# First norm's modulation columns by TensorE alone from a 128-row layout of w_mod; x tiles by two queues in turn; V begins with four row tiles

## The chip, the cores and the metric

The kernel runs on one core of a Trainium2 chip. The metric is device time in microseconds of one execution. Before the change it is 1380.65 us, the median of 3 runs (1380.23 to 1380.73). All instructions of an engine run in the order in which they are written; engines wait for each other through semaphores, and DMA transfers are issued from the queues of SyncE (SP) and ScalarE (ACT).

## The reference, cut to what matters

The input x has 2048 rows of 448. The condition c has 448 elements. With D = 448:

```
mod = (silu(c) @ w_mod).reshape(1, 6, 1, D)      # w_mod: 448 x 2688
sa, ca, ga, sb, cb, gb = mod[:, 0..5]
h = layernorm(x) * (1 + ca) + sa
q, k, v = heads of h @ wqkv                       # wqkv: 448 x 1344, 16 heads of 28
x = x + ga * (softmax(q k^T * 28**-0.5) v) @ wo
h = layernorm(x) * (1 + cb) + sb
x = x + gb * mlp(h)                               # gMLP with a spatial product
```

The change is about the first norm: its two modulation vectors sa and ca, the row tiles of x that it needs first, and the product h @ wqkv for v that follows.

## The kernel before, in words

The schedule is written out by hand: every engine executes in the order of the source. The kernel has a short beginning (norm, transposes, V, Q and K for the four groups of 512 rows), a long attention stage, an output projection, and a gMLP stage.

What happens in the first group (rows 0 to 511, four row tiles of 128):

- **Loads.** SP issues `cc_t` (c as 112 x 4, L266), then `load_x(0)` (L239; row tiles 0 and 1 go by ACT's queue, 2 and 3 together by SP), then `load_mod(0)` (L234): four tiles `wm` of 112 x 2 x 448, k = 0 to 3, each with the columns of sa and ca for 112 of the 448 rows of w_mod. Then come the four row blocks of the V part of wqkv (L250; the last block has 64 rows and is loaded twice, into both halves, by `load_z`, L145 and L146), and the next four row tiles of x.
- **Filling.** `pe_fill(n, with_)` (L288) puts n products of 128x128 that nobody reads on TensorE. Each float32 product is two LDWEIGHTS and two MATMULs in the trace, so `pe_fill(20, ones)` shows as 40 instructions. The float32r products of V show as one.
- **Norm.** VectorE takes the statistics of each row tile (L337, L338), GpSimd the reciprocal roots (L165, L166), VectorE normalizes (L348), ACT copies the last 64 columns a second time (L356). TensorE transposes (`tp_first`, L429): 8 transposes for two row tiles, 16 in all, into four banks `tp`, one for each 128 columns of h (the fourth holds the last 64 columns twice).
- **Modulation columns.** `cols["ca"]` and `cols["sa"]` hold 1+ca and sa as columns of 128 partitions. The sums over rows of w_mod are formed by ACT (k = 0, L438), VectorE (k = 1, 2, L299; the last step k = 3 in pieces, `mod_last`, L465) and then summed over the 112 partitions by TensorE with products of one moving column (`mod_dot`, L478). VectorE moves each column to SBUF (`mod_cols`, L485 and L487).
- **h and V.** For each column block c, `h_hi` (ACT, L499) writes the rounded h from `tp`, `h_full` (VectorE, L494) the full one, `h_lo` (L142) the remainder. `wv_hi` and `wv_lo` split the weight in the same way. V is the sum over 11 steps (`STEPS`), a step being one pair of an h part and a weight part; `v_step(j, kts)` (L535) does step j for the row tiles kts. Before, the first three steps run for row tiles 0 to 2 between the products for the columns c = 1 and c = 3, then for row tile 3, and then the rest for all four.
- **After V** come the products of Q and K (`qk_unit`, L381), which need the split weights of the parts "a" and "b". The tiles of part "a" reuse the buffers of `wm`, those of part "b" the buffers of the V weights, and so their loads wait until these have been read.

The same `load_mod`, `mod_acc`, `mod_split` and `mod_sum` serve the other four modulation vectors later (pairs 1 and 2).

Of the kernel before, what the change touches and what calls it, by code (L numbers as in the profile page):

```python
# [8 lines left out]
F32 = mybir.dt.float32  # L9
# [80 lines left out]
def tile_adaln_mha_gmlp(ctx, tc, x, wqkv, wo, w_in, w_spT, b_sp, w_out, cT, w_mod, out):  # L90
# [19 lines left out]
    dve.memset(ones, 1.0)  # L110
    mhalf = const.tile([128, 4], F32, name="mhalf")
    dve.memset(mhalf, -0.5)
    silu = const.tile([112, 4], F32, name="silu")
    cols = {}
    for nm in ("sa", "ca", "sb", "cb"):
        cols[nm] = const.tile([128, 4], F32, name=f"col_{nm}")
# [27 lines left out]
    def load_z(eng, dst, src):  # L144
        eng.dma_start(dst[0:64], src)  # L145
        eng.dma_start(dst[64:128], src)  # L146
# [68 lines left out]
    e2 = late_e.enter_context(tc.tile_pool(name="e2", bufs=1, side="right"))  # L215

    wv = e2.tile([128, 8, D], F32R, name="wv")
    ones_r = e2.tile([112, 128], F32R, name="ones_r")
    dve.memset(ones_r.bitcast(F32), 1.0)
    wms, xts, raws = {}, {}, {}  # L220

# [3 lines left out]
    def bank(name):  # L225
        k = mode[0](name) if mode[0] else banks[0]
        banks.remove(k)
        banks.append(k)
        return ring.tile([128, 512], F32, name=name, tag=f"b{k}")

    def load_mod(pair, eng):
        for k in range(4):
            wms[pair, k] = e1.tile([112, 2, D], F32, name="wm", tag=("wm", "wm", "raw")[pair], bufs=4)
            eng.dma_start(wms[pair, k], w_mod[:, pair, k])  # L234

    def load_x(g, eng):
        xg = e1.tile([128, 4, D], F32, name="xg")
        for t0, t1 in ((0, 1), (1, 2), (2, 4)) if g == 0 else ((0, 4),):
            (act if t1 - t0 == 1 else eng).dma_start(xg[:, t0:t1, :], x[g, :, t0:t1])  # L239
        for t in range(4):  # L240
            xts[4 * g + t] = xg[:, t, :]

# [3 lines left out]
    def load_w(kind, i, eng):  # L246
        c0, n, tag = PARTS[kind]
        raw = e1.tile([128, 2 * D], F32, name="raw", tag=tag, bufs=4)[:, :n]
        if i < 3:
            eng.dma_start(raw, wqkv[i * 128 : (i + 1) * 128, c0 : c0 + n])  # L250
        else:
            load_z(eng, raw, wqkv[384:448, c0 : c0 + n])
        raws[kind, i] = raw

    def qk_part(kind, i, eng):
# [6 lines left out]
        else:  # L262
            sub(eng, wqk[0:64, 7, cs], raw[0:64], wqk[0:64, 6, cs])

    cc_t = e1.tile([112, 4], F32, name="cc_t", bufs=1)
    sp.dma_start(cc_t, cT)  # L266
    load_x(0, sp)
    load_mod(0, sp)
# [5 lines left out]
    pool.memset(V[:, :, :, DH:32], 1.0)  # L274


    ec = e1.tile([112, 4], F32, name="ec", bufs=1)
    act.activation(ec, cc_t, AF.Exp, scale=-1.0)
    dve.tensor_scalar(out=ec, in0=ec, scalar1=1.0, scalar2=None, op0=ALU.add)
    dve.reciprocal(ec, ec)  # L280
    dve.tensor_tensor(out=silu, in0=cc_t, in1=ec, op=ALU.mult)

    pcs = {c: bank("pc") for c in (0, 2)}
    wu = bank("wu")

    def pe_fill(n, with_):
        for _ in range(n):
            pe.matmul(wu[:, 0:128], with_[:, 0:128], ones, start=True, stop=True)  # L288
# [2 lines left out]

    def mod_acc(pair, k):
        if k == 0:
            accs[pair] = e2.tile([112, 2, D], F32, name="acc")
        wm, acc = wms.pop((pair, k)), accs[pair]
        if k == 0:
            dve.tensor_scalar(out=acc, in0=wm, scalar1=silu[:, 0:1], scalar2=None, op0=ALU.mult)
        else:
            dve.scalar_tensor_tensor(out=acc, in0=wm, scalar=silu[:, k : k + 1], in1=acc, op0=ALU.mult, op1=ALU.add)  # L299

    def mod_split(pair, eng, pool_l, tag_l, bufs_l):

        acc = accs.pop(pair)
        accs[pair] = []
        for part in range(2):
            h = stage.tile([128, 512], F32R, name="acc_h", tag="qf")[0:112, :D]
            l = pool_l.tile([112, D], F32R, name="acc_l", tag=tag_l, bufs=bufs_l)
            act.activation(h, acc[:, part, :], AF.Copy)
            sub(eng, l, acc[:, part, :], h)
            accs[pair].append((h, l))  # L310
# [33 lines left out]
    def ln_norm(g, ts):  # L344
        mv, rs = mv1[g]
        for t in ts:
            xn = e1.tile([128, 512], F32, name="xn", bufs=4)
            dve.tensor_scalar(  # L348
                out=xn[:, :D],
                in0=xts.pop(4 * g + t),  # L350
                scalar1=mv[:, t, 0:1],
                scalar2=rs[:, t : t + 1],
                op0=ALU.subtract,
                op1=ALU.mult,
            )
            act.activation(xn[:, D:], xn[:, 384:D], AF.Copy)  # L356
            xn1.setdefault(g, []).append(xn)
# [56 lines left out]
    def wv_lo(i, eng):  # L414
        raw = raws.pop(("v", i))
        if i < 3:
            sub(eng, wv[:, 3 + i, :], raw, wv[:, i, :])
        else:
            sub(eng, wv[0:64, 7, :], raw[0:64], wv[0:64, 6, :])
# [7 lines left out]
    def tp_first(t):  # L427
        for c in range(4):
            pe.transpose(tps[c][:, t * 128 : (t + 1) * 128], xn1[0][t][:, c * 128 : (c + 1) * 128], ident)  # L429

    x3 = xts[3]
    pe_fill(20, ones)
    ln_stat(0, (0, 1))
    ln_rs(0, 0, 2)
    ln_stat(0, (2, 3))
    ln_rs(0, 2, 4)
    accs[0] = e2.tile([112, 2, D], F32, name="acc")
    act.activation(accs[0], wms.pop((0, 0)), AF.Copy, scale=silu[:, 0:1])  # L438
    ln_norm(0, (0, 1))
    mod_acc(0, 1)  # L440
    tp_first(0)
    tp_first(1)
    ln_norm(0, (2, 3))
    mod_acc(0, 2)
    pe_fill(5, x3)
    tp_first(2)
    tp_first(3)
    pe_fill(2, x3)

    acc0 = [stage.tile([128, 512], F32, name="acc0", tag="qh")[0:112] for _ in range(2)]  # L450
    wm3 = wms.pop((0, 3))

    def mod_last(c):
        for part in (1, 0):
            if c < 3:
                o = acc0[part][:, c * 128 : (c + 1) * 128]
                a, w = (v[:, part, c * 128 : (c + 1) * 128] for v in (accs[0], wm3))
            else:  # L460
                o = acc0[part][:, 384:512].rearrange("p (r n) -> p r n", n=64)
                a, w = (
                    v[:, part, 384:D].rearrange("p (r n) -> p r n", r=1).broadcast_to([112, 2, 64]) for v in (accs[0], wm3)
                )
            dve.scalar_tensor_tensor(out=o, in0=w, scalar=silu[:, 3:4], in1=a, op0=ALU.mult, op1=ALU.add)  # L465

    def mod_dot(c, which):
        if c == 1:
            pcs[c] = ps_o.tile([128, 512], F32, name="pc", tag="o")
        if c == 3:  # L470
            pcs[c] = pcs[1][:, 2:4]
        for i, part in enumerate((1, 0)):
            cs = slice(c * 128, (c + 1) * 128)
            if which == "C":
                o, lhs, rhs = 2 + i, wm3[:, part, cs], silu[:, 3:4]
            else:
                o, lhs, rhs = i, (accs[0][:, part] if which == "A" else acc0[part])[:, cs], ones[:112, 0:1]
            pe.matmul(pcs[c][:, o : o + 1], lhs, rhs, start=True, stop=True)  # L478

    def mod_cols(c):  # L480
        for i, (nm, plus1) in enumerate((("ca", 1.0), ("sa", 0.0))):
            o = cols[nm][:, c : c + 1]
            if c == 0:
                a, b = pcs[c][:, i : i + 1], pcs[c][:, 2 + i : 3 + i]
                dve.tensor_scalar(out=o, in0=a, scalar1=b, scalar2=plus1, op0=ALU.add, op1=ALU.add)  # L485
            else:
                dve.tensor_scalar(out=o, in0=pcs[c][:, i : i + 1], scalar1=plus1, scalar2=None, op0=ALU.add)  # L487

    def h_full(c):
        if c < 2:  # L490
            fs[c] = e1.tile([128, 512], F32, name="hfull")
        else:
            fs[c] = stage.tile([128, 512], F32, name="hfull", tag="qf")
        dve.tensor_scalar(  # L494
            out=fs[c], in0=tps[c], scalar1=cols["ca"][:, c : c + 1], scalar2=cols["sa"][:, c : c + 1], op0=ALU.mult, op1=ALU.add
        )

    def h_hi(c):
        act.activation(  # L499
# [10 lines left out]
        load_w("a", i, sp)  # L510
    wv_hi(0)
    wv_hi(2)
    mod_dot(0, "C")
    mod_dot(0, "A")
    mod_last(2)
    pe_fill(2, x3)
    mod_dot(2, "all")
    pe_fill(4, x3)
    mod_cols(0)
    h_hi(0)  # L520
    mod_cols(2)
    h_hi(2)
    mod_last(1)
    mod_last(3)
    wv_hi(1)
    wv_lo(0, dve)


    order = [STEPS[j] for j in (0, 1, 6, 2, 3, 4, 7, 5, 8, 9, 10)]
    pvs = [(kt, bank("pv") if kt < 3 else None) for kt in range(4)]  # L530

    def v_step(j, kts):
        a, b = order[j]
# [2 lines left out]
                pvs[kt][1][:, :D], hT[0][:, a, kt * 128 : (kt + 1) * 128], wv[:, b, :], start=j == 0, stop=j == NST - 1  # L536
            )

    v_step(0, (0, 1, 2))
    mod_dot(1, "all")  # L540
    mod_cols(1)
    h_hi(1)
    wv_hi(3)
    v_step(1, (0, 1, 2))
    mod_dot(3, "all")
    wv_lo(2, dve)
    h_full(0)
    mod_cols(3)
    h_hi(3)
    v_step(2, (0, 1, 2))  # L550
    pvs[3] = (3, ps_o.tile([128, 512], F32, name="pv", tag="o"))
    for j in range(3):
        v_step(j, (3,))
    h_lo(0, pool)
    h_full(2)
    h_full(1)
    wv_lo(1, dve)
    h_lo(2, dve)
    h_lo(1, dve)
    h_full(3)  # L560
    h_lo(3, dve)
    wv_lo(3, dve)
    load_x(2, sp)
    for i in (0, 2, 1, 3):
        load_w("b", i, sp)
    for j in range(3, NST):
        v_step(j, range(4))

    def qk_hi(i):
# [1042 lines left out]
```

## Time and profile before

| what | value |
|---|---|
| median of 3 runs | 1380.65 us |
| profiled execution: its own time | 1381.31 us |
| profiled execution: span of its instructions | 1379.5 us |
| TensorE busy (MATMUL) | 1373.1 us, 100% of the span |
| VectorE, ScalarE, GpSimd busy | 1072.2, 785.0, 357.8 us |
| granted TensorE clock | 1.0 |

The span is the time from the first to the last instruction of the profiled execution; 1.8 us of its own time lie around it. In the rows below PE is TensorE's MATMULs, PEld its LDWEIGHTS, DVE VectorE, ACT ScalarE, POOL GpSimd, SPq and ACTq the queues that issue DMAs. A row of the timeline has the start (us from the span's start), the length of a merged piece, engine, line, operation, output and inputs, and the number of instructions in it.

### The profile page before, as it was taken

To read this page: it belongs to the slowest core of one execution; us is meant where nothing else is said; L and a number is where in the kernel's file an instruction comes from. 1 tells how busy PE (TensorE), PEld (TensorE's weight loads), DVE (VectorE), ACT (ScalarE), POOL (GpSimd) and SP (SyncE) were. 2 spreads that over 40 slices of the span, in tenths; PEclk is the share of its full clock that TensorE was granted. 3 is DMA by queue.
4 is the path that set the end of the run, shared out by engine and by line. 5 is a ranking of instruction groups with operands and counts; after the bars stand their busy time and mean duration, and the time that the engine had idled before them with its cause. 6 is when DMAs were issued, how large, how long until landed. Compare 5 with 4: busy or idle time off the path is not lost.

```text
span 1379.5 us, 20122 instructions
## 1 busy us (share of the span) xinstructions
PE 1373.1 (100%) x7120; PEld 978.1 (71%) x7120; DVE 1072.2 (78%) x1727; ACT 785.0 (57%) x1451; POOL 357.8 (26%) x359
## 2 busy tenths in 40 slices
PE   9999999999999999999999999999999999999998
PEld 8888655555555555555555555888898888888898
DVE  7798888888888888888888880672268798889682
ACT  4724677777777777777777779364234654444221
POOL 2234324243325544633442302200042000000000
PEclk9999999999999999999999999999999999999999
DMA  8565633454244544542343321533202433335842
GB/s 253 167 157 191 201 91 111 109 157 136 89 117 122 161 121 129 156 134 90 109 122 80 108 58 49 174 141 127 85 0 76 130 100 114 116 92 179 269 160 80
DMA packets 93041, 174.56 MB, mean 127 GB/s; under 512 B 17032, under 2 KB 32010, under 8 KB 90394
## 3 DMA queue, kind: packets, MB, share of 16 engines
q1 hardware_dynamic: 90222, 168.97, 41.1%
q10 hardware_dynamic: 2718, 4.30, 0.9%
q8 instruction: 56, 0.92, 0.3%
q14 instruction: 45, 0.37, 0.1%
HBM read 111.61 MB, written 56.82 MB: 122 GB/s over the span
## 4 chain that ended last, share of the span: by engine, by line
PE 99%; DMA 0%; DVE 0%; ACT 0%; ACTq 0%; issue 0%
PE st_ps L724 19%; PE acc L1405 19%; PE o_ps L739 17%; PE mt L692 17%; PE z_ps L1297 5%; PE pq L381 5%; PE z_ps L1129 5%; PE wo_ps L995 3%; PE pv L363 2%; PE y_ps L1485 2%; PE y_ps L1484 2%; PE y_ps L1483 2%; PE tp L175 1%; PE pv L535 1%; DMA xg<-in_x_dram 0%; PE mtp L713 0%
## 5 line engine op out<-in xcount | busy, mean ns | idle before, releaser
L697 DVE TENSOR_REDUCE pm<-mt 128x1 f32<-128x512 f32 x1024 | 631.2, 682 | 86.0 <-PE mt L692 86.0
L728 ACT ACTIVATE P<-st_ps 128x512 f32<-128x512 f32 x1024 | 514.6, 631 | 202.0 <-PE st_ps L724 201.9
L724 PE MATMUL st_ps<-qst,kst 128*128 128x512 f32 x1024 | 404.5, 406 | 0.0
L692 PE MATMUL mt<-kst,qst 128*128 128x512 f32 x1024 | 402.5, 393 | 0.0
L724 PEld LDWEIGHTS st_ps<-qst,kst 128*128 128x128 f32 x1024 | 191.2, 187 | 141.3 <-issue 93.1
L739 PE MATMUL o_ps<-P,V 128*32 128x512 f32 x2048 | 247.1, 598 | 0.0
L1405 PE MATMUL acc<-wsp_h,heapA 128*128 128x512 f32 x752 | 231.5, 389 | 0.0
L692 PEld LDWEIGHTS mt<-kst,qst 128*128 128x128 f32 x1024 | 192.4, 188 | 31.6
L846 POOL TENSOR_TENSOR ws_raw<-ws_raw 128x512 f32<-128x512 f32 x124 | 159.2, 1287 | 190.8 <-DMA ws_scr<-ws_raw 129.2
L1405 PEld LDWEIGHTS acc<-wsp_h,heapA 128*128 128x128 f32 x752 | 141.2, 188 | 29.2
L1405 PE MATMUL acc<-wsp_l,heapA 128*128 128x512 f32 x376 | 146.3, 389 | 0.0
L739 PEld LDWEIGHTS o_ps<-P,V 128*32 128x32 f32 x2048 | 54.7, 109 | 123.0 <-issue 114.7
L1185 ACT ACTIVATE wsp_h<-raw_sp 128x512 fp32r<-128x512 f32 x104 | 65.6, 632 | 125.1 <-PE acc L1405 113.6
L142 DVE TENSOR_TENSOR wsp_l<-raw_sp,wsp_h 128x512 fp32r<-128x512 f32 x104 | 70.4, 686 | 16.6 <-ACT wsp_h L1185 16.4
L1405 PEld LDWEIGHTS acc<-wsp_l,heapA 128*128 128x128 f32 x376 | 70.6, 188 | 14.7
L381 PE MATMUL pq<-heapD,heapD 128*128 128x512 f32 x196 | 61.8, 390 | 0.0
L1301 DVE BATCH_NORM_STATS2 stz<-z 128x6 f32<-128x448 f32 x32 | 19.9, 626 | 44.6 <-ACT z L1300 44.5
L142 DVE TENSOR_TENSOR heapA<-z,heapA 128x1536 fp32r<-128x1536 f32 (+2 forms) x25 | 39.9, 1605 | 6.6 <-ACT heapA L1220 6.5
L1300 ACT ACTIVATE z<-z_ps 128x448 f32<-128x448 f32 x32 | 17.4, 543 | 47.4 <-PE z_ps L1297 47.4
L381 PEld LDWEIGHTS pq<-heapD,heapD 128*128 128x128 f32 x196 | 36.7, 188 | 7.5
L768 POOL TENSOR_TENSOR osb<-osb,rb 128x512 f32<-128x512 f32 x15 | 19.3, 1290 | 87.0 <-DMA rb<-r_scr 77.8
L1484 PE MATMUL y_ps<-wouts,uT 128*128 128x448 f32 x112 | 40.9, 365 | 0.0
(220 smaller groups left out, 1438.7 us busy)
## 6 DMA issues: line engine op xcount, KB each, us to landing
ws_scr<-ws_raw SPq DMA_DIRECT2D x92, 256.0 KB
raw_sp<-ws_scr SPq DMA_DIRECT2D x92, 256.0 KB
ws_raw<-in_w_spT_dram SPq DMA_DIRECT2D x72, 256.0 KB
kst<-qk_scr SPq DMA_DIRECT2D x45, 224.0 KB
qst<-qk_scr SPq DMA_DIRECT2D x45, 224.0 KB
qk_scr<-qh SPq DMA_DIRECT2D x28, 256.0 KB
qk_scr<-ql SPq DMA_DIRECT2D x28, 256.0 KB
z_scr<-z1t SPq DMA_DIRECT2D x28, 256.0 KB
```

The lines of the kernel that those rows point to most:

```text
L142: eng.tensor_tensor(out=dst, in0=a, in1=hi.bitcast(F32), op=ALU.subtract)
L381: pe.matmul(pq, wqk[:, b, m * 128 : (m + 1) * 128], hT[g][:, a, :], start=j == 0, stop=j == NST - 1)
L692: pe.matmul(mt, qst[h % 3][:, t * 128 : (t + 1) * 128], kst[h % 3][:, kb * 512 : (kb + 1) * 512], start=True, stop=True)
L697: dve.tensor_reduce(out=pms[h][:, t, kb : kb + 1], in_=mt, axis=AX.X, op=ALU.max)
L724: pe.matmul(st, kst[h % 3][:, kt * 128 : (kt + 1) * 128], qst[h % 3][:, qb * 512 : (qb + 1) * 512], start=True, stop=True)
L728: act.activation(p, st, AF.Exp, scale=SCALE)
L739: pe.matmul(otile[h][32 * qb : 32 * qb + 32, :], V[:, kt, h, :], ptiles.pop((u, qb)), start=kt == 0, stop=kt == NT - 1)
L846: pool.tensor_tensor(out=ws_tile(op[0]), in0=ws_tile(op[2]), in1=ws_tile(op[4]), op=ALU.add if op[3] == "+" else ALU.subtract)
L1129: pe.matmul(ps_t, w1[:, b, f * 128 : (f + 1) * 128], h2T[g][:, a, :], start=j == 0, stop=j == NST - 1)
L1297: pe.matmul(ps_t[:, :D], h2T[g][:, a, tt * 128 : (tt + 1) * 128], w2[:, b, hf * D : (hf + 1) * D], start=j == 0, stop=j == NST - 1)
L1405: pe.matmul(a[j], z[:, c], w, start=start and k == 0, stop=st == 3 and k == 2, skip_group_check=not new or j == 3)
L1484: pe.matmul(y[:, :D], uT[k][:, 7 + f, ts], wouts[0][:, f, :], start=False, stop=False)
```

## The change

- The host lays w_mod out in 128 rows: three tiles (k = 0, 1, 2) of 128 x 2 x 448, and a fourth with 448 columns in which the last 64 rows of w_mod stand for sa in partitions 0 to 63 and for ca in partitions 64 to 127. c is laid out as 128 x 4 to match, with its last 64 elements in both halves, and `silu` is 128 x 5: columns 3 and 4 hold the last 64 elements in the one and the other half, with zeros elsewhere. wqkv gets its last 64 rows twice on the host, so that its last block is one load of 128 rows.
- The columns sa and ca come from TensorE alone. `mod_dot(k)` multiplies the 128-column blocks of `wm` with the k-th column of `silu` and adds up over k in one bank `pc0`. The fourth block has 64 columns and is multiplied twice, into partitions 0 to 63 and 64 to 127. That makes 10 products for each of k = 0, 1, 2 and 5 for k = 3 (with two moving columns there). VectorE then moves all four columns of ca, and all four of sa, in one instruction each. `mod_last` and `mod_cols` are gone.
- The four row tiles of x are four loads: 0 and 2 by ACT's queue, 1 and 3 by SP's.
- The order on TensorE is: 26 fill products (20 before), `mod_dot(0)`, `mod_dot(1)`, the transposes of row tiles 0 and 1, `mod_dot(2)`, the transposes of 2 and 3, `mod_dot(3)`, 5 fill products, and then all 11 steps of V, each for four row tiles. `h_full` for c = 1 and 3 moves from VectorE to ACT. Steps 2 and 6 of V change places.
- For the later pairs `mod_acc` takes the last k in two halves.

```diff
-    silu = const.tile([112, 4], F32, name="silu")
+    silu = const.tile([128, 5], F32, name="silu")
+    pool.memset(silu, 0.0)
...
     def load_mod(pair, eng):
         for k in range(4):
-            wms[pair, k] = e1.tile([112, 2, D], F32, name="wm", tag=("wm", "wm", "raw")[pair], bufs=4)
-            eng.dma_start(wms[pair, k], w_mod[:, pair, k])
+            n = 2 if k < 3 else 1
+            wms[pair, k] = e1.tile([128, 2, D], F32, name="wm", tag=("wm", "wm", "raw")[pair], bufs=4)[:, :n]
+            eng.dma_start(wms[pair, k], w_mod[:, pair, 2 * k : 2 * k + n])
...
-        for t0, t1 in ((0, 1), (1, 2), (2, 4)) if g == 0 else ((0, 4),):
-            (act if t1 - t0 == 1 else eng).dma_start(xg[:, t0:t1, :], x[g, :, t0:t1])
+        for t0, t1 in ((0, 1), (1, 2), (2, 3), (3, 4)) if g == 0 else ((0, 4),):
+            (act if g == 0 and t0 % 2 == 0 else eng).dma_start(xg[:, t0:t1, :], x[g, :, t0:t1])
...
-        if i < 3:
-            eng.dma_start(raw, wqkv[i * 128 : (i + 1) * 128, c0 : c0 + n])
-        else:
-            load_z(eng, raw, wqkv[384:448, c0 : c0 + n])
+        eng.dma_start(raw, wqkv[i * 128 : (i + 1) * 128, c0 : c0 + n])
...
-    dve.tensor_tensor(out=silu, in0=cc_t, in1=ec, op=ALU.mult)
-    pcs = {c: bank("pc") for c in (0, 2)}
+    for r0, r1, a, o in ((0, 128, 0, 3), (0, 64, 3, 1), (64, 128, 3, 1)):
+        b = a + r0 // 64
+        dve.tensor_tensor(out=silu[r0:r1, b : b + o], in0=cc_t[r0:r1, a : a + o], in1=ec[r0:r1, a : a + o], op=ALU.mult)
...
+    pc0 = ps_o.tile([128, 512], F32, name="pc", tag="o")
+
+    def mod_dot(k):
+        wm = wms.pop((0, k))
+        for c in range(4):
+            for part in range(2 if k < 3 else 1):
+                w = wm[:, part, c * 128 : min(D, (c + 1) * 128)]
+                v = silu[:, k : k + 1] if k < 3 else silu[:, 3:5]
+                for r in (slice(0, 128),) if c < 3 else (slice(0, 64), slice(64, 128)):
+                    o = pc0[r, 2 * c + part : 2 * c + part + 1] if k < 3 else pc0[r, 2 * c : 2 * c + 2]
+                    pe.matmul(o, w, v, start=k + c + part == 0, stop=k == 3, skip_group_check=True)
+
-    pe_fill(20, ones)
+    pe_fill(26, ones)
     ln_stat(0, (0, 1))
     ln_rs(0, 0, 2)
     ln_stat(0, (2, 3))
     ln_rs(0, 2, 4)
-    accs[0] = e2.tile([112, 2, D], F32, name="acc")
-    act.activation(accs[0], wms.pop((0, 0)), AF.Copy, scale=silu[:, 0:1])
+    mod_dot(0)
+    mod_dot(1)
     ln_norm(0, (0, 1))
-    mod_acc(0, 1)
     tp_first(0)
     tp_first(1)
+    mod_dot(2)
     ln_norm(0, (2, 3))
-    mod_acc(0, 2)
-    pe_fill(5, x3)
     tp_first(2)
     tp_first(3)
-    pe_fill(2, x3)
+    mod_dot(3)
+    pe_fill(5, ones)
...
     wv_hi(0)
     wv_hi(2)
-    mod_dot(0, "C")
-    mod_dot(0, "A")
-    mod_last(2)
-    pe_fill(2, x3)
-    mod_dot(2, "all")
-    pe_fill(4, x3)
-    mod_cols(0)
+    wv_lo(0, dve)
+    for nm, part, plus1 in (("ca", 1, 1.0), ("sa", 0, 0.0)):
+        dve.tensor_scalar(out=cols[nm], in0=pc0[:, part:8:2], scalar1=plus1, scalar2=None, op0=ALU.add)
     h_hi(0)
-    mod_cols(2)
+    h_full(0)
     h_hi(2)
-    mod_last(1)
-    mod_last(3)
+    h_lo(0, pool)
+    wv_lo(2, dve)
     wv_hi(1)
-    wv_lo(0, dve)
-    order = [STEPS[j] for j in (0, 1, 6, 2, 3, 4, 7, 5, 8, 9, 10)]
-    pvs = [(kt, bank("pv") if kt < 3 else None) for kt in range(4)]
+    h_hi(1)
+    h_full(2)
+    wv_hi(3)
+    h_hi(3)
+    wv_lo(1, dve)
+    h_full(1, act)
+    h_lo(2, dve)
+    h_full(3, act)
+    h_lo(1, dve)
+    h_lo(3, dve)
+    wv_lo(3, dve)
+    order = [STEPS[j] for j in (0, 1, 2, 6, 3, 4, 7, 5, 8, 9, 10)]
+    pvs = [(kt, bank("pv") if kt < 3 else ps_o.tile([128, 512], F32, name="pv", tag="o")) for kt in range(4)]
...
     load_x(2, sp)
     for i in (0, 2, 1, 3):
         load_w("b", i, sp)
-    for j in range(3, NST):
+    for j in range(NST):
         v_step(j, range(4))
```

More of the change, by code (lines that the diff above doesn't have):

```diff
@@ L217, in tile_adaln_mha_gmlp @@
     wv = e2.tile([128, 8, D], F32R, name="wv")
-    ones_r = e2.tile([112, 128], F32R, name="ones_r")
+    ones_r = e2.tile([128, 128], F32R, name="ones_r")
     dve.memset(ones_r.bitcast(F32), 1.0)
@@ L263, in qk_lo @@
             sub(eng, wqk[0:64, 7, cs], raw[0:64], wqk[0:64, 6, cs])
-    cc_t = e1.tile([112, 4], F32, name="cc_t", bufs=1)
+    cc_t = e1.tile([128, 4], F32, name="cc_t", bufs=1)
     sp.dma_start(cc_t, cT)
@@ L274, in tile_adaln_mha_gmlp @@
     pool.memset(V[:, :, :, DH:32], 1.0)
-    ec = e1.tile([112, 4], F32, name="ec", bufs=1)
+    ec = e1.tile([128, 4], F32, name="ec", bufs=1)
     act.activation(ec, cc_t, AF.Exp, scale=-1.0)
@@ L293, in mod_acc @@
         if k == 0:
-            accs[pair] = e2.tile([112, 2, D], F32, name="acc")
+            accs[pair] = e2.tile([128, 2, D], F32, name="acc")
         wm, acc = wms.pop((pair, k)), accs[pair]
@@ L297, in mod_acc @@
             dve.tensor_scalar(out=acc, in0=wm, scalar1=silu[:, 0:1], scalar2=None, op0=ALU.mult)
-        else:
-            dve.scalar_tensor_tensor(out=acc, in0=wm, scalar=silu[:, k : k + 1], in1=acc, op0=ALU.mult, op1=ALU.add)
+            return
+        for r, w, o, i in [(slice(0, 128), wm, acc, k)] if k < 3 else [
+            (slice(64 * part, 64 * part + 64), wm[:, 0], acc[:, part], 3 + part) for part in range(2)
+        ]:
+            dve.scalar_tensor_tensor(out=o[r], in0=w[r], scalar=silu[r, i : i + 1], in1=o[r], op0=ALU.mult, op1=ALU.add)
     def mod_split(pair, eng, pool_l, tag_l, bufs_l):
@@ L305, in mod_split @@
         for part in range(2):
-            h = stage.tile([128, 512], F32R, name="acc_h", tag="qf")[0:112, :D]
-            l = pool_l.tile([112, D], F32R, name="acc_l", tag=tag_l, bufs=bufs_l)
+            h = stage.tile([128, 512], F32R, name="acc_h", tag="qf")[:, :D]
+            l = pool_l.tile([128, D], F32R, name="acc_l", tag=tag_l, bufs=bufs_l)
             act.activation(h, acc[:, part, :], AF.Copy)
@@ L429, in tp_first @@
             pe.transpose(tps[c][:, t * 128 : (t + 1) * 128], xn1[0][t][:, c * 128 : (c + 1) * 128], ident)
-    x3 = xts[3]
-    pe_fill(20, ones)
+    pc0 = ps_o.tile([128, 512], F32, name="pc", tag="o")
[9 more added lines that the diff above has]
+    pe_fill(26, ones)
     ln_stat(0, (0, 1))
@@ L436, in tile_adaln_mha_gmlp, with h_full @@
     ln_rs(0, 2, 4)
-    accs[0] = e2.tile([112, 2, D], F32, name="acc")
-    act.activation(accs[0], wms.pop((0, 0)), AF.Copy, scale=silu[:, 0:1])
+    mod_dot(0)
+    mod_dot(1)
     ln_norm(0, (0, 1))
-    mod_acc(0, 1)
     tp_first(0)
     tp_first(1)
+    mod_dot(2)
     ln_norm(0, (2, 3))
-    mod_acc(0, 2)
-    pe_fill(5, x3)
     tp_first(2)
     tp_first(3)
-    pe_fill(2, x3)
[L450 to L489, printed above, removed]
+    mod_dot(3)
+    pe_fill(5, ones)
+    def h_full(c, eng=dve):
         if c < 2:
@@ L493, in h_full @@
             fs[c] = stage.tile([128, 512], F32, name="hfull", tag="qf")
-        dve.tensor_scalar(
-            out=fs[c], in0=tps[c], scalar1=cols["ca"][:, c : c + 1], scalar2=cols["sa"][:, c : c + 1], op0=ALU.mult, op1=ALU.add
-        )
+        mul, add = cols["ca"][:, c : c + 1], cols["sa"][:, c : c + 1]
+        if eng is act:
+            act.activation(fs[c], tps[c], AF.Identity, scale=mul, bias=add)
+        else:
+            eng.tensor_scalar(out=fs[c], in0=tps[c], scalar1=mul, scalar2=add, op0=ALU.mult, op1=ALU.add)
     def h_hi(c):
@@ L537, in v_step @@
             )
[L539 to L562, printed above, removed]
     load_x(2, sp)
@@ L1587 @@
     from concourse.bass_utils import run_bass_kernel_spmd as _run
+    wm = _np.asarray(inputs["w_mod"]).reshape(448, 3, 2, 448)
     lay = {
         "x": _np.asarray(inputs["A_x"])[0].reshape(4, 4, 128, 448).transpose(0, 2, 1, 3),
-        "wqkv": inputs["A_wqkv"],
+        "wqkv": _np.asarray(inputs["A_wqkv"])[[*range(448), *range(384, 448)]],
         "wo": inputs["A_wo"],
@@ L1596 @@
         "w_out": inputs["B_w_out"],
-        "cT": inputs["c"].reshape(4, 112).T,
-        "w_mod": _np.asarray(inputs["w_mod"]).reshape(4, 112, 3, 2, 448).transpose(1, 2, 0, 3, 4),
+        "cT": _np.asarray(inputs["c"]).reshape(7, 64)[[0, 1, 2, 3, 4, 5, 6, 6]].reshape(4, 128).T,
+        "w_mod": _np.concatenate([wm[:384].reshape(3, 128, 3, 2, 448).transpose(1, 2, 0, 3, 4).reshape(128, 3, 6, 448),
+                                  wm[384:].transpose(2, 0, 1, 3).reshape(128, 3, 1, 448)], axis=2),
     }
```

## The prediction

> **What bounds the kernel now.** First the page's head, then busy time by stretch, to see where a shift of any engine reaches the end.
>
> ```profile
> span 1379.5 us, 20122 instructions
> PE 1373.1 (100%) x7120; PEld 978.1 (71%) x7120; DVE 1072.2 (78%) x1727; ACT 785.0 (57%) x1451; POOL 357.8 (26%) x359
> ...
> 0.00:18.30 18.30, 15.62 (x108) 15.06 (x108) 11.55 (x35) 6.97 (x13) 5.63 (x14) 1.00 0.92 265
> 18.30:26.30 8.00, 7.99 (x39) 7.35 (x40) 7.83 (x18) 3.54 (x7) 1.30 (x1) 1.00 0.89 277
> 26.30:110.00 83.70, 83.70 (x410) 72.62 (x409) 71.68 (x113) 42.27 (x82) 24.54 (x22) 1.00 0.63 175
> 110.00:860.00 750.00, 750.00 (x4160) 441.41 (x4159) 625.88 (x1054) 523.17 (x1037) 288.09 (x279) 1.00 0.41 119
> ```
>
> From 18.3 us on TensorE (the first busy number behind the length) has no gap to absorb anything: V ends at 26.31, and what shifts that moment shifts the end of the kernel by as much. So the whole question is when V ends. The chain of waits shows what sets it now (start, length, what):
>
> ```profile
> 16.84 0.35 PE pc L478 x4
> ...
> 17.22 0.04 DVE col_ca L487
> ...
> 17.29 0.16 DVE col_sa L487
> ...
> 17.48 0.79 ACT heapD L499
> ...
> 18.31 8.01 PE pv L535 x38
> 26.31 5.04 PE pq L381 x22
> 38.10 4.48 PE pv L363 x22
> ```
>
> 38 of V's 44 products run in 8.01 us behind the columns of c = 1; a product in a full stream costs 4.48/22 = 0.204 us. A V of 44 without a gap is 8.01 + 6 x 0.204 = 9.23 us. Before, V's last 9.23 us would begin at 17.08: that is the start to beat.
>
> **The change part by part.** 1. *TensorE's queue ahead of V.* It is served in order, so it has to be added up. Rows of the LDWEIGHTS timeline (the first two from views that end and begin near 6 us):
>
> ```profile
> 1.03 5.16 PEld L288 LDWEIGHTS wu<-ones 128*128 128x128 f32 x24 [1.03 <-DVE ones L110]
> ...
> 6.11 1.87 PEld L288 LDWEIGHTS wu<-ones 128*128 128x128 f32 x16
> 9.72 0.86 PEld L429 LDWEIGHTS tp<-ident,xn 128*128 128x128 f32 x8 [1.75 <-DVE xn L348]
> ...
> 13.29 0.52 PEld L478 LDWEIGHTS pc<-silu,wm 112*128 112x128 f32 x4 [0.22 <-DMA wm<-in_w_mod_dram]
> 13.72 0.53 PEld L478 LDWEIGHTS pc<-ones,acc 112*128 112x128 f32 x4
> 14.17 0.53 PEld L288 LDWEIGHTS wu<-ones,xg 128*128 128x128 f32 x4
> 14.62 0.53 PEld L478 LDWEIGHTS pc<-ones,acc 112*128 112x128 f32 x4
> ```
>
> Fill passes come every 5.16/24 = 0.21 us until about 6.1 and every (1.87-0.19)/15 = 0.112 after that (0.19 is the length of one). The 40th pass of the fill begins at 7.79. Twelve more (26 products instead of 20) end at 7.79 + 13 x 0.112 = 9.25. Before, TensorE then stood idle for 1.75 us waiting for the norm; now it goes straight on.
>
> A column product costs the same as a fill product although it moves one column only: from 13.29 to 14.17 there are eight passes, 0.11 each. Two passes for a product make 0.22 us. The view of line 478 shows the pairs: the two products for c = 0 are these x4.
>
> `mod_dot(k)`, k < 3: six products of 128 columns, 12 x 0.112 = 1.34 us, and four of 64 columns, 8 passes. `mod_dot(3)`: 6 passes = 0.67, and 4 of 64 columns. The trace has no load of 64 columns. The nearest rows are these:
>
> ```profile
> L724 PEld LDWEIGHTS st_ps<-qst,kst 128*128 128x128 f32 x1024 | 191.2, 187 | 141.3 <-issue 93.1
> L739 PEld LDWEIGHTS o_ps<-P,V 128*32 128x32 f32 x2048 | 54.7, 109 | 123.0 <-issue 114.7
> ...
> 153.76 0.23 PE st_ps L724
> 153.99 0.26 PE mt L692
> 154.25 1.85 PE o_ps L739 x16
> 156.10 0.43 PE st_ps L724
> 156.54 0.24 PE mt L692
> ```
>
> A load of 32 columns is 187-109 = 78 ns shorter than one of 128, 0.81 ns a column; 64 columns save 52 ns, so a pass is 0.06 us (an estimate). And going from the 128*128 form to the narrow one and back has a price: 0.26 and 0.43 stand where 0.23 is usual, 0.03 + 0.20. [...] So the 64-column part costs 8 x 0.06 + 0.15 = 0.63 (k < 3) and 0.24 + 0.15 = 0.39 (k = 3). Bounds: below, 0.10 and 0.05, if the two halves run side by side and the switch is hidden; above, 8 x 0.112 + 0.23 = 1.13 and 0.68. `mod_dot` is then 1.97 (1.44 to 2.47), and for k = 3 1.06 (0.72 to 1.35).
>
> [...]
>
> Transposes: 8 in 0.87 us (0.86 from the row at 9.72), 1.74 for 16, as before.
>
> Sum: 9.25 + 1.97 + 1.97 + 0.87 + 1.97 + 0.87 + 1.06 = **17.96 us** for the end of `mod_dot(3)` in the queue (16.1 to 19.8 by the bounds). Before, the columns for c = 1 left TensorE at 17.19 (16.84 + 0.35), with six products of V done.
>
> 2. *From the last column product to V.* Four loads from 14.62 fill the queue to 15.07; their products end at 15.23 (row below), 0.16 later. Then 0.04 to VectorE, 0.23 for two columns, 0.03 to ACT, 0.79 for `h_hi(0)`, 0.04 to TensorE: 1.29 us. Moving four columns at once instead of one I cost at nothing more: 128x1 takes 0.15.
>
> ```profile
> 14.73 0.50 PE L478 MATMUL pc<-ones,acc 112*128 112x1 f32 x4
> 15.27 0.16 DVE L487 TENSOR_SCALAR col_ca<-pc 128x1 f32<-128x1 f32 x1 [0.54 <-PE pc L478]
> ```
>
> V starts at 17.96 + 1.29 = 19.25 and ends at 19.25 + 9.23 = 28.48. The five fill products (1.12 us) lie inside the 1.29 and cost nothing; without them TensorE would be idle there. **28.48 - 26.31 = +2.2 us** (+0.3 to +4.0).
>
> 3. *Does V stall?* A step is 4 x 0.204 = 0.81 us. Durations (mean ns behind the bar's busy time):
>
> ```profile
> L494 DVE TENSOR_SCALAR hfull<-tp,col_ca,col_sa 128x512 f32<-128x512 f32 x4 | 3.1, 804 | 0.0
> L499 ACT ACTIVATE heapD<-tp,col_sa,col_ca 128x512 fp32r<-128x512 f32 x4 | 3.1, 777 | 1.4 <-DVE col_sa L487 0.8 <-DVE col_sa L485 0.5
> L142 DVE TENSOR_TENSOR wv<-raw,wv 128x448 fp32r<-128x448 f32 x3 | 1.8, 616 | 0.0
> L142 DVE TENSOR_TENSOR heapD<-hfull,heapD 128x512 fp32r<-128x512 f32 x2 | 1.3, 686 | 0.0
> L412 ACT ACTIVATE wv<-raw 128x448 fp32r<-128x448 f32 x3 | 1.7, 571 | 1.4 <-DMA raw<-in_wqkv_dram 1.4
> ```
>
> ACT from V's start: `h_hi(2)` 0.78 (wanted by the second step at 0.81), `wv_hi(1)` 1.35, `h_hi(1)` 2.13 (wanted at 2.44), `wv_hi(3)` 2.70, `h_hi(3)` 3.47, `h_full(1)` 4.25, `h_full(3)` 5.03. VectorE ends `h_lo(1)` at 4.94 (wanted at 6.5), `h_lo(3)` at 5.72 (7.3), `wv_lo(3)` at 6.33 (8.1). No stall; the two `h_full` that move to ACT have room there. The split that the products of Q and K need follows 0.7 us earlier against V's end than before, when `wv_lo(3)` ended 2.2 us ahead of it.
>
> 4. *Loads.* The 112-row and 64-row transfers are slow (last number, GB/s; 5.0 to 11.5 carries mostly `wm`, 13.5 to 15.0 the two 64-row halves, the others 128 rows):
>
> ```profile
> 2.20:5.00 2.80, 2.80 (x15) 2.80 (x14) 1.38 (x5) 0.94 (x2) 1.35 (x2) 1.00 1.02 362
> 5.00:11.50 6.50, 4.94 (x40) 4.75 (x39) 4.42 (x11) 1.56 (x3) 2.19 (x4) 1.00 1.04 248
> 13.50:15.00 1.50, 1.50 (x16) 1.50 (x15) 0.80 (x4) 0.75 (x2) 0.03 (x1) 1.00 1.14 249
> 15.00:18.00 3.00, 3.00 (x25) 2.91 (x24) 2.59 (x11) 2.36 (x4) 0.52 (x1) 1.00 0.98 358
> ```
>
> With 128 rows I expect about 360 throughout: the 1.61 MB of `wm` save 1.61/0.248 - 1.61/0.360 = 2.0 us, so the last tile lands near 11.2 instead of 13.27. But TensorE reaches `mod_dot(3)` at 16.9 only. Even at the old landing times no product would wait, so this gain, x in turn by two queues, and the sums that leave VectorE and ACT are worth nothing: what they shorten isn't what ends last, TensorE's queue is. Should that shrink, they set the time (first rival). Of what is issued: ACT's queue has two loads of x as before; SP's gets one more for x and loses one for each last weight block; GpSimd clears `silu` once and VectorE writes it in three small instructions instead of one, all ahead of 5 us, while TensorE fills until 9.25. The loads of part "a" now wait for `mod_dot` instead of for VectorE; the last goes out when `mod_dot(3)` is done, near 18, and the products of Q and K that want it begin at 28.5.
>
> **Sum.** The profiled execution took 1381.31 us; +2.2 makes 1383.5. The median of the runs lies 0.66 below it: **1382.8 us**, 0.16% slower. What this kernel's measurement can tell from no change is about 0.2%, 2.8 us, so the forecast itself counts as the same.
>
> One unknown has no second row: the moment when the passes become fast (6.1 here). Fast from the start, the fill would end 24 x 0.1 = 2.4 us sooner; slow to the end, 28 x 0.1 = 2.8 later. Before, the idle time ahead of the transposes hid 1.7 us of this; now nothing does. [...]
>
> **The rivals.** *A, faster: the loads set V's start.* If the products of `mod_dot` were hidden, V would wait for the last tile: 11.2 + 1.06 + 1.29 = 13.5, 5.7 us earlier than I say, and the time 1380.65 + 2.2 - 5.7 = 1377.1. For it: the loads do get shorter. It takes 30 products and 16 transposes in the 1.9 us between 9.25 and 11.2, against 0.11 us a pass measured: 7%, part way included. *B, slower for certain: the narrow products cost as much as full ones and each switch its full price.* Upper bounds: +4.0, 1384.7; it decides from 0.9 us a `mod_dot` for the 64-column part. For it speaks 0.43 in place of 0.23; against it the shorter load of 32 columns. 22%. *C, about equal: the halves run side by side.* +0.3 to +1.2, 1381.4. For it: sixteen narrow products of 512 columns take only 1.85 us, 0.116 each. 21%. *D: the layout doesn't speed up the loads.* Same time as the forecast, by point 4; no chance of its own.
>
> **How the numbers follow.** Forecast (+1.2 to +3.1): 50%; A 7%, B 22%, C 21%. The range 1380.9 to 1385.0 leaves out A and the worst of B. Slower by over 0.2% (+2.8): B and a fifth of the forecast, 32%; faster by over 0.2%: 7%; the same 61%.
>
> **What would show it.** Right: TensorE without a gap from its first fill to V, `mod_dot` about 2 us each, V's first product near 19.3, 44 in 9.2 us, every `wm` landed before its products. Wrong: TensorE waiting for a DMA ahead of a `mod_dot`, V before 17.1, a gap inside V, or 64-column passes far from 0.06 us.

## The result, and the profile after

| | before | after |
|---|---|---|
| median of the runs | 1380.69 us (1380.23 to 1380.84, 4 runs) | 1387.84 us (1387.42 to 1388.16, 4 runs) |
| profiled execution: its own time, span | 1381.31 us, 1379.5 us | 1388.16 us, 1386.3 us |
| end of V in it | 26.31 us | 33.31 us |

The changed kernel is slower by 7.15 us: ratio 1.0052, interval 1.0035 to 1.0070. The forecast was 1382.8 us in a range up to 1385.0, so the time lies outside the range. Slower is what its sum had said, by 2.2 us. V ends 7.0 us later, and the span is 6.8 us longer: all of it arises before V's end, as the prediction said it would have to.

The chain of waits of the changed kernel from the start to the first products of Q and K (start us, length us, what):

```profile
1.04 8.06 PE wu L288 x52
9.10 3.51 PE pc L444 x40
12.61 1.90 PE tp L432 x8
14.51 2.87 PE pc L444 x20
17.38 1.90 PE tp L432 x8
19.28 1.38 PE pc L444 x10
20.66 2.43 PE wu L288 x10
23.09 10.22 PE pv L517 x44
33.31 5.01 PE pq L384 x22
```

Apart from the first 1.04 us only TensorE stands in it, with no gap from the first fill on, as forecast. But look at equal work in it (a pass is one weight load with its product): `mod_dot(0)` and `mod_dot(1)` take 3.51 us for 40 passes, 0.088 each; `mod_dot(2)` takes 2.87 for 20, 0.144 each. Eight transposes take 1.90 us where the kernel before needs 1.09 and 0.87 in its chain. From about 12 us on everything is slow. The busy time by stretch shows why (the granted clock is the first number behind the last bracket, after it the DMA share and GB/s):

```profile
9.00:10.00 1.00, 1.00 (x12) 1.00 (x11) 0.82 (x2) 0.40 (x2) 0.00 (x0) 1.00 1.04 380
10.00:11.00 1.00, 1.00 (x16) 0.97 (x15) 0.00 (x0) 0.11 (x1) 0.00 (x0) 1.00 1.06 398
11.00:12.00 1.00, 1.00 (x10) 1.00 (x10) 0.20 (x1) 0.58 (x1) 0.18 (x1) 1.00 1.13 441
12.00:12.50 0.50, 0.50 (x9) 0.48 (x9) 0.42 (x1) 0.00 (x0) 0.50 (x1) 0.57 1.07 444
12.50:13.00 0.50, 0.50 (x5) 0.48 (x5) 0.00 (x0) 0.00 (x0) 0.34 (x1) 0.50 0.89 373
...
24.00:25.00 1.00, 1.00 (x4) 0.90 (x3) 1.00 (x2) 1.00 (x3) 0.34 (x1) 0.50 0.99 417
25.00:26.00 1.00, 1.00 (x4) 0.90 (x4) 0.98 (x2) 1.00 (x3) 0.00 (x0) 0.64 0.98 365
26.00:27.00 1.00, 1.00 (x6) 0.93 (x6) 0.94 (x3) 1.00 (x3) 0.00 (x0) 1.00 0.71 194
```

The granted clock falls to one half at 12.07 us (0.57 over half a us: full for 0.07) and comes back at 25.72 (0.64 over one us: full for the last 0.28). That is 13.65 us at half clock, over the column products, the transposes, the last fill and the first part of V. TensorE counts as 100% busy all through it.

One thing to know when reading this column: it doesn't show the slow start. The first fill passes of both kernels come 0.21 us apart and then 0.112, and the rows of that stretch show 1.00 before and behind. In the changed kernel a weight load of the first fill takes 0.331 us up to 5 us (mean of 19) and 0.192 from 6.5 to 8.5; one of the last fill, at a granted 0.50, takes 0.328. Ahead of the first change in the column, the clock has to be read from the length of the passes.

The loads did what point 4 expected. ACT's first V weight now waits for its DMA until 11.19 us, before until 13.71:

```profile
11.19 0.58 ACT L415 ACTIVATE wv<-raw 128x448 fp32r<-128x448 f32 x1 [1.08 <-DMA raw<-in_wqkv_dram]
```

### The profile page after: what moved, and what is told of

Read it like the earlier page. It is cut to its first block, busy times and chain, and to the rows that moved or that the text cites. A ratio compares the mean times of both kernels' runs of the same rounds, so it can differ in the third digit from the quotient of the medians.

```text
span 1386.3 us, 20194 instructions
## 1 busy us (share of the span) xinstructions
PE 1381.7 (100%) x7166; PEld 986.5 (71%) x7166; DVE 1067.2 (77%) x1715; ACT 784.9 (57%) x1452; POOL 358.6 (26%) x360
## 4 chain that ended last, share of the span: by engine, by line
PE 100%; DVE 0%; issue 0%
PE st_ps L682 19%; PE acc L1363 18%; PE o_ps L697 17%; PE mt L650 17%; PE z_ps L1255 5%; PE pq L384 5%; PE z_ps L1087 5%; PE wo_ps L953 3%; PE pv L366 2%; PE y_ps L1442 2%; PE y_ps L1443 2%; PE y_ps L1441 2%; PE tp L176 1%; PE wu L288 1%; PE pv L517 1%; PE pc L444 1%
```

## The experiments

**The theory.** What the clock follows is how much the products stream: a long stretch of products with one moving column lowers it although the engine is never idle. A pass with 128 columns of weights takes about 0.11 us whether it moves 1 or 128 columns (the rows of the prediction's point 1), but with one column it streams next to nothing. The kernel before has such products too, but only in groups of four or eight passes between fill products and V.

**Rivals.** R1: what lowers the clock are the changes of form between 128*128 and the 64-column products. R2: the cause lies outside TensorE; the loads just then reach 441 GB/s.

### More moving columns: wide64

```diff
-                v = silu[:, k : k + 1] if k < 3 else silu[:, 3:5]
+                v = silu[:, k : k + 1].broadcast_to([128, 64]) if k < 3 else silu[:, 3:5].rearrange("p (a n) -> p a n", n=1).broadcast_to([128, 2, 64])
...
-                    o = pc0[r, 2 * c + part : 2 * c + part + 1] if k < 3 else pc0[r, 2 * c : 2 * c + 2]
+                    i = 64 * (2 * c + part)
+                    o = pc0[r, i : i + 64] if k < 3 else pc0[r, i : i + 2 * 64].rearrange("p (a n) -> p a n", n=64)
...
-        dve.tensor_scalar(out=cols[nm], in0=pc0[:, part:8:2], scalar1=plus1, scalar2=None, op0=ALU.add)
+        dve.tensor_scalar(out=cols[nm], in0=pc0[:, 64 * part : 512 : 128], scalar1=plus1, scalar2=None, op0=ALU.add)
```

> The changed kernel with 64 moving columns in each product of mod_dot (the same column of silu repeated 64 times; the columns of pc0 then stand 64 apart) instead of one. Nothing else differs. Theory (the clock gate counts a stretch of one-column products as rest, and so halved the clock at 12.07 us): the granted clock stays 1.0 after the first fill, mod_dot stays at about 1.65 us, V starts near 17.8 and ends near 27.0, time 1381.4. Rival R1 (the changes of form between 128*128 and 64-column products are what the gate sees as rest) and rival R2 (something outside TensorE, such as the loads at over 400 GB/s, lowers the clock): the clock halves again near 12 us, V ends near 33.3, time 1387.8.

Measured: 1382.69 us, against 1379.85 for the kernel before on that chip; ratio 1.0020 (1.0011 to 1.0030). Its chain of waits, and two stretches of it:

```profile
1.04 7.98 PE wu L288 x52
9.02 3.53 PE pc L445 x40
12.55 1.02 PE tp L432 x8
13.57 1.67 PE pc L445 x20
15.24 1.02 PE tp L432 x8
16.26 1.04 PE pc L445 x10
17.30 1.31 PE wu L288 x10
18.62 9.13 PE pv L518 x44
27.74 5.01 PE pq L384 x22
```

```profile
9.00:12.50 3.50, 3.50 (x42) 3.23 (x40) 1.46 (x3) 1.09 (x3) 0.63 (x1) 1.00 1.06 410
12.50:18.60 6.10, 6.10 (x59) 5.59 (x57) 0.34 (x3) 0.92 (x2) 0.38 (x1) 1.00 0.67 233
```

The clock holds (1.00 in both stretches), with the same loads at 410 GB/s (406 in the changed kernel from 9 to 12 us) and the same changes of form. Forty passes with 64 columns take 3.53 us; with one column they took 3.51, the last 0.54 of them at half clock. At full clock the columns cost little: the twenty passes behind the first transposes take 1.67 us here and 1.56 with one column (wide_first2, below). V ends at 27.74 instead of 33.31, so 5.57 of the 7.0 us are the clock's. R1 and R2 expected 1387.8 and fall. The time is 1.3 us above the 1381.4 that the theory gave, for two reasons. V's end is 0.7 later than I had put it. And I had added V's shift to the median of the kernel before, though its profiled execution, from which the shift was read, lies 0.66 above that median; wide64's lies only 0.21 above its own.

### No 64-column form: one_form

```diff
-                w = wm[:, part, c * 128 : min(D, (c + 1) * 128)]
+                w = wm[:, part, min(c * 128, D - 128) : min(D, (c + 1) * 128)]
...
-                for r in (slice(0, 128),) if c < 3 else (slice(0, 64), slice(64, 128)):
+                for r in (slice(0, 128),):
```

> The changed kernel, where the fourth block of mod_dot is one product with the last 128 columns (320 to 447) of w_mod instead of two with 64: partitions 0 to 63 of the fourth modulation column then hold the wrong columns. No 64-column form and no change of form is left; the products still move one column. Theory: still throttled, 16 passes in each mod_dot at half clock instead of 12 and 8 narrow ones, about 0.9 us more: 1388.7. R1: the clock holds, V starts near 18.2 and ends near 27.5, time 1381.9. R2: as the theory.

Measured: 1388.33 us, ratio 1.0060 (1.0045 to 1.0075). In this kernel partitions 0 to 63 of the fourth modulation column hold other columns of w_mod; it leaves out the right ones.

```profile
10.00:12.00 2.00, 2.00 (x17) 2.00 (x16) 0.26 (x1) 0.68 (x2) 0.25 (x1) 0.80 1.08 417
12.00:14.00 2.00, 2.00 (x11) 2.00 (x11) 0.36 (x1) 0.00 (x0) 0.78 (x1) 0.50 1.00 411
...
24.00:26.00 2.00, 2.00 (x9) 1.79 (x9) 1.98 (x3) 2.00 (x5) 0.90 (x1) 0.79 0.97 398
```

Without any change of form the clock falls all the same, at 11.2 us, and comes back at 24.84: again 13.64 us. V ends at 33.18 on the chip on which wide64 ended it at 27.74. R1 falls a second time.

### Thin fill products in the kernel before: before_thin_fill

```diff
-            pe.matmul(wu[:, 0:128], with_[:, 0:128], ones, start=True, stop=True)
+            pe.matmul(wu[:, 0:1], with_[:, 0:128], ones[:, 0:1], start=True, stop=True)
```

> The kernel before, whose fill products move one column instead of 128 (nobody reads them). Theory: the clock isn't released by the first fill and stays at one half until V has run for a while; fills, transposes and column products ahead of V take 0.21 us a pass, time 1387 to 1390. R1 and R2: fills of one column serve as well as those of 128, the clock rises at about 6 us, time 1380.7.

Measured: 1389.41 us, ratio 1.0068 (1.0051 to 1.0085). Nothing but the number of columns that nobody reads was changed, and it costs 9.6 us. From its chain of waits:

```profile
1.04 8.69 PE wu L288 x40
9.73 1.81 PE tp L429 x8
...
15.92 1.71 PE pc L478 x8
...
24.98 9.36 PE pv L535 x38
34.35 5.02 PE pq L381 x22
```

Forty passes take 8.69 us (0.22 each), eight column passes 1.71 (1.05 before). The clock column reads 1.00 up to 30 us in this run, as it does ahead of the first change in the changed kernel; by the length of the passes the clock stays low from the start until V has run for a while: the weight loads of the fills take 0.333 us (median) from the first to the last one, at 20.6 us. In the kernel before they take 0.192 from 6.1 us on. There the fill products are what raises the clock, and it is their columns that do it.

### Where the bound lies: wide16, wide32, wide_first2

wide16 and wide32 are wide64 with 16 and 32 in place of 64.

> As wide64, with 16 moving columns instead of 64 in each product of mod_dot. Where is the bound? If the gate goes by the share of time in which columns stream, 16 columns in a pass of 0.112 us are an eighth of what a fill product streams, and the clock halves near 12 us as with one column: 1387.8. If it takes any product of more than a few columns as work, the clock holds: a little faster than wide64's 1382.7, since the 64-column blocks take less, near 1382.2.

Measured: 1388.33 us, ratio 1.0059 (1.0044 to 1.0074): 16 columns are no better than one.

```profile
10.00:12.00 2.00, 2.00 (x20) 1.94 (x17) 0.38 (x1) 0.69 (x2) 0.35 (x1) 0.77 1.08 413
12.00:14.00 2.00, 2.00 (x16) 1.96 (x16) 0.24 (x1) 0.00 (x0) 0.65 (x1) 0.50 1.01 414
```

> As wide64 and wide16, with 32 moving columns. 64 held the clock (1382.7) and 16 didn't (1388.3); this halves the interval. If the clock holds, 1382.4; if it halves near 12 us, 1388. A pass is 0.112 us whatever it moves, and 32 columns are a quarter of a fill product.

Measured: 1384.43 us as a median, but no execution took that long. Of ten, five took 1380.94 to 1381.67 us with a mean clock of 1.0, and five 1387.19 to 1388.50 with 0.995 or 0.996. So 32 columns lie at the bound, and which side an execution falls on isn't set by the program, which is the same in all ten.

wide_first2 moves 64 columns in `mod_dot(0)` and `mod_dot(1)`, and one (two for k = 3) in the others, which lie between and behind the transposes (the columns of `pc0` change to match). It asks whether the clock holds over these others:

```diff
-                v = silu[:, k : k + 1].broadcast_to([128, 64]) if k < 3 else ...
+                v = silu[:, k : k + 1].broadcast_to([128, 64]) if k < 2 else silu[:, k : k + 1] if k < 3 else silu[:, 3:5]
```

> As wide64, but only mod_dot(0) and mod_dot(1) move 64 columns; mod_dot(2) and mod_dot(3), which lie between the transposes, move one column (two for k = 3). [...]

Measured: 1382.33 us, ratio 1.0017 (1.0008 to 1.0026): the clock holds, with a mean of 1.0 in all ten executions.

```profile
12.94 1.02 PE tp L432 x8
13.96 1.56 PE pc L445 x20
15.52 1.02 PE tp L432 x8
16.55 0.78 PE pc L445 x10
```

```profile
12.70:16.10 3.40, 3.40 (x42) 3.30 (x39) 0.00 (x0) 0.00 (x0) 0.09 (x1) 1.00 0.79 292
```

Between 12.94 and 17.33 TensorE does nothing but 16 transposes (2.04 us) and products of one or two columns (2.34 us), and that is enough to hold the clock: the row reads 1.00, and eight transposes take 1.02 us where they took 1.90 at half clock. These 4.4 us are longer than the 2.97 us of column products, from 9.10 to 12.07, behind which it fell in the changed kernel. So with transposes among them, the products of one or two columns did not lower the clock here; their longest stretch without a transpose is 1.56 us.

### With the clock held, is the queue's length what is left? wide64_fill20

```diff
-    pe_fill(26, ones)
+    pe_fill(20, ones)
```

> As wide64, with 20 fill products ahead of mod_dot(0) instead of 26. Theory (the clock holds and TensorE's queue alone sets V): everything 12 passes of 0.112 us earlier, V ends near 25.7, time 1380.0, a little under the kernel before. R1 and R2: half clock, V's end near 32 or later, time over 1386.

Measured: 1381.80 us, ratio 1.0014 (1.0005 to 1.0024).

```profile
1.04 6.74 PE wu L288 x40
7.78 3.67 PE pc L445 x40
...
17.51 9.14 PE pv L518 x44
26.65 5.04 PE pq L384 x22
```

V ends 1.09 us before wide64's, for 12 passes less (1.24 by the chain's first rows). So TensorE's own queue sets V's start, as point 1 said. The time is 1.8 us above what I expected, for the reasons given at wide64 (V's end is 0.95 later than 25.7, and this profiled execution lies 0.27 below its median). The kernel isn't faster than the one before: column products and transposes take 8.42 us of TensorE from 7.78 on. In this trace none of them waits for a load; how much earlier they could begin wasn't tried.

### The new loads without the new sums: dve_sums and dve_sums2

The layout in 128 rows and the order of the loads stay. The sums over k = 0 to 2 go back to ACT and VectorE; TensorE takes the fourth tile and the sum over partitions, with 64 moving columns, c = 0 and 2 first.

```diff
-    mod_dot(0)
-    mod_dot(1)
...
+    act.activation(accs[0], wms.pop((0, 0)), AF.Copy, scale=silu[:, 0:1])
+    ln_norm(0, (2, 3))
+    mod_acc(0, 1)
+    mod_acc(0, 2)
...
+    for c in (0, 1, 2, 3):
+        mod_w3(c)
+    for c in (0, 2, 1, 3):
+        mod_rest(c)
```

`mod_w3(c)` multiplies block c of the fourth tile with `silu[:, 3:5]`; `mod_rest(c)` adds the sum of `accs[0]` over the partitions on top, as products with ones.

> The changed kernel's loads and layout alone: k = 0 to 2 are summed by ACT and VectorE as in the kernel before, TensorE takes only the fourth tile and the sum over partitions (4 + 8 products of 64 moving columns, 2 more for each halved block), with the columns for c = 0 and 2 first in a bank of their own; 24 fill products ahead, 2 and 2 and 2 between. Theory (loads that end 2.7 us earlier are worth something once TensorE's queue isn't what ends last): VectorE's last sum near 12.1, V starts near 14.3 and ends near 23.5, time 1378.5, below the 1379.9 of the kernel before. If the loads are worth nothing even then: 1380 or above.

Measured: 1379.34 us against 1380.16, ratio 0.9994 (0.9985 to 1.0002): not told apart from the kernel before. V ended at 25.09, not 23.5. Most of that lies ahead of V, which starts at 15.70 and not at 14.3. The chain of waits goes back to the fourth w_mod tile, behind which come 4.23 us of column and fill products:

```profile
3.53 7.80 DMA wm<-in_w_mod_dram
...
11.47 1.28 PE pc L448 x10
...
15.70 0.53 PE pv L539 x2
```

A row of its timeline shows a smaller loss inside V:

```profile
16.26 8.45 PEld L539 LDWEIGHTS pv<-wv,heapD 128*128 128x128 f32 x42 [0.32 <-DVE hfull L494]
```

V's third product waited for VectorE to read the bank of the first transposes, which the third row tile had been given, 0.32 us. dve_sums2 mends this, takes out two of the fill products, and moves the columns for c = 1 and 3 ahead of the first `h_full`:

```diff
-    pvs = [(kt, bank("pv") if kt < 3 else ps_o.tile([128, 512], F32, name="pv", tag="o")) for kt in range(4)]
+    pvs = [(0, bank("pv")), (1, bank("pv")), (2, ps_o.tile([128, 512], F32, name="pv", tag="o"))]
+    banks.remove(5)
+    banks.insert(0, 5)
+    pvs.append((3, bank("pv")))
...
-    pe_fill(2, ones)
     for c in (0, 2, 1, 3):
         mod_rest(c)
...
+    mod_cols(1)
     h_hi(0)
     h_full(0)
-    mod_cols(1)
```

> As dve_sums, with two things mended that its trace shows: TensorE stood 0.3 us in V because the third row tile's bank was that of the first transposes, which VectorE had not read yet (here it takes the bank of the columns instead), and VectorE moved the columns for c = 1 and 3 only after h_full(0); and the two fill products ahead of the sums over k are gone. If what is left sets V's end as I read it: first product near 15.0, no gap in V, V's end near 24.2 instead of 25.1, time 1378.5, clearly under the kernel before. If VectorE's last sum or the landing of the fourth w_mod tile (which varies by some tenths of a us from run to run) ends last: as dve_sums, 1379.3.

Measured: 1378.05 us against 1379.40, ratio 0.9990 (0.9981 to 0.9999).

```profile
11.15 1.04 PE pc L448 x10
12.19 1.87 PE pc L453 x20
14.06 0.64 PE wu L288 x4
14.70 9.10 PE pv L541 x44
23.80 4.99 PE pq L384 x22
```

V ends at 23.80 us. The fourth w_mod tile landed at 11.33 us in dve_sums (3.53 + 7.80); here its products begin at 11.15, behind the transposes. This version is 1.35 us faster than the kernel before; the interval just excludes no change. It differs from that kernel in more than the loads: the fourth w_mod tile goes through TensorE, V runs in one piece, and two `h_full` are ACT's. So it shows what the change is worth once TensorE's queue ahead of V is short, and that the loads are what pays there is argued, not shown.

## Why the prediction was wrong, point by point

**What bounds the kernel, and what V's end is worth: right.** V's end moved by 7.0 us, the span by 6.8.

**Point 1 is the step that failed**, in the sentence that a column product costs the same as a fill product although it moves one column only, 0.11 us a pass. It was read from eight passes between fills, and was then multiplied by 70, of which 40 stand in one run. In that run the price holds (3.51 us, even less than the 3.94 I had added up), but the clock falls near its end: half clock from 12.07 to 25.72. The sum has every term behind the fill at full clock, and puts what these products do to the clock at nothing, without a reason. The rows show it term by term, predicted and measured: `mod_dot(0)` and `(1)` 3.94 and 3.51; transposes 0.87 and 1.90, twice; `mod_dot(2)` 1.97 and 2.87; `mod_dot(3)` 1.06 and 1.38; from there to V 1.29 and 2.43; V 9.23 and 10.22. With the fill's end at 9.10 instead of 9.25 these add up to the 4.83 us between 28.48 and 33.31. I had treated the clock as a matter of when it rises only, behind the sum; no rival had it fall. Its signs of being wrong didn't catch this either: TensorE waited for no load, and V had no gap and didn't begin early. wide64, which changes the number of moving columns alone, takes back 5.57 of the 7.0 us. (The lower bound of the sum, 16.1, adds up to 16.0; nothing hangs on it.)

**The narrow products: the price was too high.** The first two `mod_dot` take 3.53 us in wide64, 1.76 each, not 1.97; the first one of the changed kernel, all at full clock, takes 1.76 by its weight loads (from 8.83 to 10.59). No run shows the 0.15 us that the sum takes for a round trip between the forms. What the runs showed is the whole: 1.76 less 12 passes of 0.112 leaves 0.42 us for the eight loads of 64 columns with both changes of form, where the sum has 0.63. The full price in rival B isn't what made the kernel slow: one_form has none of these products and is as slow (1388.33 us against 1387.84).

**With the clock held, the sum was near.** V's end in wide64 is 27.74 against 28.48 forecast: the column products are shorter (6.24 us in place of 6.97), the transposes longer (2.04 in place of 1.74). wide64 takes 1382.69 us, the forecast said 1382.8. That is an agreement in part by luck: the kernel before ran 0.8 us faster on that chip. Against it wide64 is 2.84 us slower, where the forecast was 2.2 and V's end in the two traces differs by 1.43; where the kernel before ends V on that chip wasn't traced.

**Point 2, the five fill products at no cost: wrong at half clock.** They take 2.43 us, and their cover, the way from the last column product to V, is shorter: `h_hi(0)` begins at 21.04 and takes half of the 1.44 us in this row of the changed kernel's timeline, so the first operand of V is there by 21.8, and V's products begin at 22.74, behind the fill. At full clock the point nearly holds: in wide64 `h_hi(0)` begins at 17.68 (ACT is busy for the last 0.32 us of the stretch that ends at 18.00) and would end near 18.4 at the 0.72 us it takes in the changed kernel, an estimate; in the chain V follows the fill at 18.62.

```profile
21.04 1.44 ACT L475 ACTIVATE heapD<-tp,col_sa,col_ca 128x512 fp32r<-128x512 f32 x2 [9.27 <-DVE col_sa L491]
22.74 10.57 PE L517 MATMUL pv<-wv,heapD 128*128 128x448 f32 x44
```

**Point 3: right.** V's 44 products run without a gap; 9.13 us in wide64.

**Point 4: right in its conclusion.** From 6 to 14 us the loads run at 364 to 419 GB/s, in stretches of 2 us, where about 360 was expected. The first V weight is there 2.5 us sooner. VectorE's statistics of the second row tile of x begin at 5.19 us, before at 6.97. None of that shortened the changed kernel. dve_sums2 is faster where TensorE isn't in the way. How much of that is the 128-row layout and how much the turn of the queues for x wasn't tried.

**The rivals.** A, B and C were all three priced at full clock; the kernel went the way of none. TensorE has no gap in the changed kernel's trace from the first fill on, and the clock fell all the same, from 1.00 to 0.50 at 12.07 us, in a stretch of products of one column.

## What to carry to other kernels

Where many small products stand in a row, ask what they stream and not how busy TensorE looks: here forty passes took 3.53 us with 64 columns and 3.51 with one, and the 64 kept the full clock where one column lost 5.6 us. Price a group of instructions from a row taken at its own length: eight passes between other work did not show what forty in a row do to the clock. And before work moves to the engine that ends last, add up its queue: of all these versions, the only one clearly faster than the kernel before is one in which the sums went back to the engines that had time.

## What the runs showed of the hardware that was not expected

- **The clock went with the columns streamed.** In a stretch of 3.5 to 4 us of passes of 0.09 to 0.1 us, the granted clock fell from 1.00 to 0.50 with 1 and 16 moving columns and stayed at 1.00 with 64; with 32 it stayed in five of ten executions (mean clock 1.0, in the others 0.995 or 0.996). What decides between the two at 32 isn't shown.
- **A fall lasted the same time in four kernels.** Changed kernel, one_form, wide16 and wide32 all stayed at half clock for 13.64 to 13.65 us (wide16 from 11.08 to 24.72). The order of the work was the same in all four, but the fall met it at different places, and the rise came 1.3 to 2.6 us into V. The four runs agree; what sets the length isn't shown.
- **It took more to raise the clock than to hold it.** In before_thin_fill V has six products at 21.04 and 23.01 us, 1.33 us for each three, and the passes stay slow until the full V has run from 24.98 to about 28 (an estimate from its 38 products in 9.36 us, at 0.44 and then 0.204 each). Yet 2.04 us of transposes in 4.4 us hold the clock in wide_first2. In before_thin_fill 16 transposes, 3.62 us between 9.73 and 15.27, did not raise it.
- **When the first fill raises the clock** differs between the traces of these kernels, by the length of the fill: the first 52 passes took 7.59 us (wide16) to 8.37 (wide_first2).

```profile
1.04 8.37 PE wu L288 x52
```
